# Six PSUM banks: three tiles of two banks each, or two-bank tiles in attention and one-bank tiles after it

## The chip, the cores and the metric

The kernel runs on one core of a Trainium2 chip. The metric is the device time of one execution in microseconds (us), the median of several executions. The engines are TensorE (PE, the matrix products; its weight loads are listed apart as PEld), VectorE (DVE), ScalarE (ACT), GpSimd (POOL) and SyncE (SP, which here issues DMAs).

## The reference

Attention feeds one mixture-of-experts-like layer, and that feeds a second one. All data are float32.

```python
def _attn_ref(q, k, v):                      # 2 x 12 heads x 448 x 64
    scores = scale * np.matmul(q, k.transpose(0, 1, 3, 2))
    scores = np.where(mask, -1000000000.0, scores)          # causal
    scores = scores - np.max(scores, axis=-1, keepdims=True)
    attn = np.exp(scores)
    attn = attn / (np.sum(attn, axis=-1, keepdims=True) + 1e-09)
    return np.matmul(attn, v)

def _moe_ref(x, w_in, w_out):                # 896 x 768, 768 x 2048, 2048 x 768
    r = np.maximum(x @ w_in, 0.0)
    return (r * r) @ w_out

def _moe2_ref(x, w1, w2, w3, w_out):         # 768 x 768 each
    h = np.maximum(np.maximum(x @ w1, x @ w2), x @ w3)
    return h @ w_out

x = attn_out.transpose(0, 2, 1, 3).reshape(896, 768)
return _moe2_ref(_moe_ref(x, ...), ...)
```

## The kernel before

**Stages.** The attention works on 12 pairs of heads. The two layers follow as four stages of block products: x by `w_in` (blocks f0 to f7, the "first stage" here), the squares by the first `w_out` (blocks o0 to o7, class `Second`, the second stage), that by w1, w2 and w3 with the maximum taken (blocks h0 to h8, the third stage), and the last `w_out`, whose products are partly in the order and partly in fixed code behind it (lines 1118 to 1179). Stages overlap: the first products of f0 and f1 stand between the last heads.

**Products.** Each block of two by two sub-blocks is computed with seven products M1 to M7 of sums of operands instead of eight plain ones, and each operand is a high and a low part, so that every product is three passes (`PASSES`): high by high, high by low, low by high. M1 to M7 of one block are 9 matmuls each of 128x448 (3 passes, 3 steps of depth), written by `matmul_in_parts` (L581). Beside a product stand the steps that feed it: a quarter of a weight is read as it came or summed (T), its high part is made by a copy on ACT (H, L199) or POOL (H', L289), its low part by a subtraction on DVE (L, `dve_lo`, L202). These quarters sit in a ring of five buffers (`wq`). Raw weights are cast (C on ACT, C' on POOL) and joined (J, DVE), and J sets the next load going. The steps that empty a bank are V: ACT copies (`keep`, L613, and L618, which goes from one bank into another), ACT relu and square (L640), or sums on DVE (`dve`, L212).

**PSUM.** The memory that PE writes has eight banks here. Six are held as three tiles of two banks each: pp0 (banks 0 and 1), pp2 (2 and 3), pp4 (4 and 5); banks 6 and 7 are tiles of their own, ps6 and ps7. In attention a pair holds the scores of one query block for both heads, or the transposed probabilities, which ACT or DVE copies out in one instruction over both banks (`place`, L499); the last pair of heads uses pp2 and pp4 alone for the latter. Afterwards the products use all eight banks singly, the six as halves of the pairs:

- the first stage gives each block three banks, b, c and d: even blocks 6, 1, 0 and odd ones 2, 4, 3; M5 and M3 go to c, M2 to d, the others to b;
- the second stage uses banks 5, 7, 6 (B) and 0, 1, 3 (C), the third 2, 5, 4 for even and 6, 7, 1 for odd blocks;
- the fixed code at the end uses 0, 3, 1 (`bb`), 7, 2, 5 (`cc`) and 4, 6 (`rest`).

**Order.** Nothing is scheduled by the compiler. `ORDER` is a string of 1776 step names, run one after the other (L1108); each engine gets its instructions in that order and runs them one after the other. Between instructions that use the same tile the layer below puts semaphore waits: a reader waits for the writer, and a writer waits for the readers before it. It does that by tile, so the halves of pp2 count as one thing in it. The names in the string: s scores, m mask and minimum (DVE, L450), e exponential (ACT, L458), a guard of the sum (DVE, a' on POOL, L465), r reciprocal, n norm (POOL, n' DVE, L473), g transposes (L484), h place, w product with V (L509), x and d operands of the first stage, then C, J, T, H, L, M and V as above, S, XH, XL and Y the second stage's operands and results, Z and W those of the last. A mark ' is the other engine for the same step; the number is the pair of heads, or the block.

Of the kernel before, what the change touches and what calls it, by code (L numbers as in the profile page):

```python
# [8 lines left out]
F32 = mybir.dt.float32  # L9
# [19 lines left out]
s2.0 m2.0 s0.0 m3.0 e2.0 e3.0 s4.0 m1.0 s6.0 m0.0 e1.0 m4.0 m5.0 a1'.0 r1.0 e4.0 e5.0 m6.0 s2.1  # L29
e0.0 n2.0 n3.0 s0.1 m2.1 m0.1 s6.1 m1.1 e6.0 m3.1 a2.0 g1.0 a0'.0 s4.1 m6.1 r0.0 n6.0 n4'.0 s6.2  # L30
g3.0 n5.0 m4.1 r2.0 e0.1 e1.1 h1.0 g0.0 e3.1 a2'.1 m5.1 e6.1 r2.1 e5.1 m6.2 n1.1 h3'.0 n1.0 n0.0
s4.2 m4.2 e4.1 h0.0 m5.2 a0'.1 r0.1 n0'.1 e6.2 n5.1 s6.3 g2.0 e2.1 e4.2 a1'.1 s0.2 h2'.0 s2.2 m0.2
s0.3 m1.2 e5.2 e0.2 n4.1 m2.2 g2.1 n6.1 m3.2 m1.3 a0'.2 m0.3 h2.1 w0.0 g0.1 e0.3 r1.1 n2'.1 r0.2
s4.3 h0'.1 n3.1 e1.3 s2.3 e3.2 m4.3 m5.3 g1.1 w1.0 e2.2 w2.0 w3.0 m3.3 m2.3 a1.2 n6.2 e1.2 h1.1
g3.1 g3.2 wload n4.2 e3.3 a2'.3 n5.2 r1.2 a2'.2 n2.2 e5.3 r2.2 g0.2 h3.1 e4.3 m6.3 n0.2 n3.2 s6.4
h3'.2 g1.2 s2.4 h0.2 h1.2 xh'.0 s0.4 xl.0 xf'.0 n1.2 e2.3 g2.2 r2.3 w0.1 a1'.3 m3.4 e6.3 e3.4 m2.4
m0.4 r1.3 e2.4 m6.4 h2.2 a0'.3 s4.4 m1.4 n2.3 e0.4 s2.5 n3.3 n0'.3 e6.4 g1.3 a1'.4 w1.1 n1.3 w2.1
w3.1 m4.4 r0.3 m2.5 e4.4 n4.3 n6.3 e1.4 m3.5 s6.5 n5'.3 a2'.4 m5.4 g2.3 h1'.3 g3.3 e5.4 h2.3 r1.4
r2.4 d3.1 h3.3 g0.3 s4.5 C'.i0 h0.3 a0'.4 n2.4 3h'.1 m6.5 n0.4 s0.5 w0.2 e6.5 w1.2 n1'.4 w2.2 r0.4
w3.2 m4.5 n6.4 m1.5 m5.5 e4.5 m0.5 e3.5 J.i0 n3.4 n4.4 n5.4 e1.5 xh'.2 e5.5 g1.4 e2.5 a1'.5 g2.4  # L40
h1'.4 s6.6 a0.5 xf.2 xl.2 h2.4 r1.5 r0.5 g3.4 3l.1 h3.4 g0.4 s2.6 n2.5 n3.5 h0.4 e0.5 a2'.5 s4.6
s0.6 m2.6 m3.6 m4.6 m0.6 g1.5 m5.6 r2.5 n5.5 n4.5 n1'.5 e3.6 w0.3 w1.3 w2.3 n6.5 m6.6 e2.6 w3.3
m1.6 d2.3 g3.5 h3'.5 d1.3 n0.5 h1.5 e4.6 g0.5 e1.6 C'.i2 e0.6 xh.3 a1'.6 a2'.6 1h'.3 h0.5 g2.5
s6.7 e6.6 s2.7 h2.5 s4.7 m6.7 xl.3 e5.6 s0.7 w0.4 m3.7 r1.6 w1.4 r2.6 w2.4 n3.6 n2'.6 m2.7 n1.6
e3.7 m4.7 m5.7 n0'.6 w3.4 s0.8 a0'.6 e6.7 g2.6 e2.7 m1.7 e5.7 a1'.7 m0.7 r0.6 g1.6 2h'.3 r1.7 e1.7
xh'.4 m1.8 m0.8 e0.7 h2.6 n5.6 d4.3 s6.8 s2.8 n4.6 s4.8 n6.6 h1.6 m2.8 e0.8 xf.4 m3.8 e4.7 g0.6
h0.6 xl.4 g3.6 w0.5 m5.8 a2'.7 a0'.7 n2.7 r0.7 e1.8 4h'.3 w1.5 e2.8 m4.8 w2.5 r2.7 w3.5 e3.8 h3.6
a2'.8 n4'.7 n5.7 1l.3 e5.8 s4.9 m6.8 d3.5 r2.8 J.i2 a1'.8 n3.7 g0.7 m5.9 r1.8 s6.9 n6.7 m4.9 e6.8
g3.7 n1.7 n0'.8 e4.8 3h'.5 n0.7 n2.8 h0.7 a0.8 r0.8 H'.f0M1 h3.7 w0.6 g2.7 n3'.8 g1.7 s2.9 e4.9
m6.9 n1.8 2l.3 n6.8 e5.9 n4.8 h2.7 h1.7 H'.f1M1 w1.6 w2.6 w3.6 m2.9 3l.5 m3.9 s0.9 g1.8 e6.9 s2.10  # L50
a0'.9 m1.9 xh.6 m0.9 xl.6 r0.9 m3.10 n5.8 h1.8 e1.9 e0.9 m2.10 n6'.9 H'.f1M2 s6.10 a2'.9 g3.8
C'.i1 s4.10 xf.6 h3.8 g2.8 g0.8 L.f1M1 e3.9 m6.10 w0.7 e3.10 e2.10 w1.7 r2.9 m5.10 n4.9 m4.10 w2.7
# [97 lines left out]
def tile_attention_moe_moe(  # L150
# [23 lines left out]
    nc = tc.nc  # L174
# [455 lines left out]
    class First(Sevens):  # L630
# [596 lines left out]
```

## Time and profile before

| | |
|---|---|
| median of 3 runs | 462.77 us (462.5 to 462.91) |
| profiled execution | 461.83 us, span of its profile 460.0 us |
| busy share of the span | PE 96%, DVE 85%, PEld 82%, ACT 63%, POOL 31% |
| mean granted clock of TensorE | 1.000 of full speed |
| DMA | 61.04 MB, mean 133 GB/s |

The span runs from the first instruction to the last; the time on record has 1.83 us more. Matmuls are pipelined and a row's duration includes some of the row before, so a busy PE is not a PE at its peak. An engine's busy share is a mean over stages with different limits; the windows below cut the span into stages.

### The profile page before, as it was taken

The page shows a single profiled execution, that of the slowest core. Times are in us where ns is not written, and L with a number is a line of the kernel's source. Part 1 is how long each engine was busy: PE and PEld are TensorE (multiplying, and loading weights), DVE is VectorE, ACT ScalarE, POOL GpSimd, SP SyncE. Part 2 cuts the span into 40 slices and gives each one's busy share as a digit, 9 for nine tenths or more (in the row PEclk, how much of TensorE's full clock was granted, in tenths as well). Part 3 has the DMA queues.
Part 4 walks back from the last instruction along what each step waited for, and adds up shares of the span by engine and source line. Part 5 has one row for each costly group of instructions (what it writes and reads, how often), then busy time and mean ns, then how long its engine had stood idle before and what let it go on. Part 6 is the DMA issues. An engine that isn't in the chain of part 4 may idle for free.

```text
span 460.0 us, 7587 instructions
## 1 busy us (share of the span) xinstructions
PE 441.3 (96%) x2585; PEld 378.0 (82%) x2585; DVE 392.1 (85%) x845; ACT 289.4 (63%) x652; POOL 143.2 (31%) x223
## 2 busy tenths in 40 slices
PE   8999999999899999999999999999999999899986
PEld 5555556888798998988999889888998999798986
DVE  6998998997777678989998999999898887779762
ACT  6998997756665798978756764763444443512541
POOL 4786998031012032234384113004221111100000
PEclk9999999999999999999999999999999999999999
DMA  7565553464764354896957552036273420000114
GB/s 222 175 192 166 177 185 93 146 198 137 207 176 118 122 152 129 223 212 178 186 87 146 196 200 76 27 111 205 70 216 126 139 68 2 0 1 0 51 37 154
DMA packets 42854, 61.04 MB, mean 133 GB/s; under 512 B 2112, under 2 KB 35008, under 8 KB 42816
## 3 DMA queue, kind: packets, MB, share of 16 engines
q1 hardware_dynamic: 39072, 55.61, 39.1%
q0 software_dynamic: 3456, 4.72, 6.5%
q8 instruction: 20, 0.33, 0.3%
q10 hardware_dynamic: 288, 0.23, 0.1%
q14 instruction: 18, 0.15, 0.1%
HBM read 53.08 MB, written 2.75 MB: 121 GB/s over the span
## 4 chain that ended last, share of the span: by engine, by line
PE 76%; ACT 9%; DVE 6%; POOL 4%; issue 2%; DMA 1%; ACTq 0%; POOLq 0%; SPq 0%; DVEq 0%
PE pp L581 43%; PE ps L581 21%; PE pp L1019 5%; ACT pr L458 4%; POOL pr L473 3%; PE ps L509 2%; PE pp L439 1%; DMA wr<-in_moe_w 1%; DVE wq L202 1%; ACT ph L499 1%; PE pp L484 1%; PE ps L1019 1%; DVE wd L273 1%; DVE z L212 1%; ACT up L263 1%
## 5 line engine op out<-in xcount | busy, mean ns | idle before, releaser
L581 PE MATMUL pp<-s,wq 128*128 128x448 f32 (+1 forms) x405 | 87.7, 364 | 5.4 <-ACT pp L618 2.9
L581 PEld LDWEIGHTS pp<-s,wq 128*128 128x128 f32 x405 | 74.0, 188 | 14.0 <-ACT pp L618 4.0
L581 PE MATMUL pp<-x,wq 128*128 128x448 f32 (+1 forms) x318 | 71.1, 365 | 1.2 <-DVE wq L202 1.1
L581 PE MATMUL pp<-a,wq 128*128 128x448 f32 x315 | 69.3, 368 | 1.8 <-ACT s L613 1.8
L289 POOL CAST wq<-wd 128x384 fp32r<-128x384 f32 x38 | 33.8, 890 | 107.1 <-PE ps L581 43.7
L581 PEld LDWEIGHTS pp<-x,wq 128*128 128x128 f32 x318 | 58.3, 188 | 8.6 <-DVE wq L202 2.9
L581 PEld LDWEIGHTS pp<-a,wq 128*128 128x128 f32 x315 | 58.7, 188 | 7.7 <-issue 1.5
L202 DVE TENSOR_TENSOR wq<-wd,wq 128x384 fp32r<-128x384 f32 x99 | 57.3, 591 | 7.6 <-ACT wq L199 5.3
L273 DVE SCALAR_TENSOR_TENSOR wd<-wr,up 128x768 int32<-128x768 int32 x56 | 55.0, 982 | 5.8 <-ACT up L263 4.2
L289 POOL CAST wq<-wt 128x384 fp32r<-128x384 f32 x29 | 17.0, 587 | 118.0 <-PE ps L581 46.8
L202 DVE TENSOR_TENSOR wq<-wt,wq 128x384 fp32r<-128x384 f32 x68 | 38.7, 581 | 11.5 <-POOL wq L289 7.2
L581 PE MATMUL ps<-s,wq 128*128 128x448 f32 (+1 forms) x224 | 48.3, 361 | 0.0
L458 ACT ACTIVATE pr<-pr,st 128x384 f32<-128x384 f32 (+3 forms) x84 | 43.8, 526 | 3.3 <-DVE st L450 3.3
L199 ACT CAST wq<-wd 128x384 fp32r<-128x384 f32 x61 | 31.0, 513 | 23.3 <-PE pp L581 14.6
L581 PE MATMUL ps<-x,wq 128*128 128x448 f32 (+1 forms) x200 | 44.4, 358 | 0.0
L581 PEld LDWEIGHTS ps<-s,wq 128*128 128x128 f32 x224 | 40.6, 188 | 4.0 <-DVE s L202 0.3
L473 POOL TENSOR_SCALAR pr<-pr,st 128x256 f32<-128x256 f32 (+3 forms) x68 | 41.4, 622 | 5.2 <-DVE st L469 4.0
L263 ACT CAST up<-wr 128x768 f16<-128x768 bf16 x27 | 29.2, 1083 | 21.5 <-DVE wd L273 7.6
L581 PEld LDWEIGHTS ps<-x,wq 128*128 128x128 f32 x200 | 36.4, 188 | 2.8
L581 PE MATMUL ps<-a,wq 128*128 128x448 f32 x144 | 32.2, 367 | 0.0
L450 DVE CUSTOM_DVE_ANT_0 pr<-pp,mask 128x384 f32<-128x384 f32 (+2 forms) x72 | 27.3, 416 | 4.9 <-PE pp L439 4.6
L199 ACT CAST wq<-wt 128x384 fp32r<-128x384 f32 x39 | 19.9, 513 | 17.0 <-PE pp L581 8.7
(166 smaller groups left out, 790.3 us busy)
## 6 DMA issues: line engine op xcount, KB each, us to landing
wr<-in_moe_w_out SPq DMA_DIRECT2D x22, 768.0 KB, 4.5
wr<-in_moe_w SPq DMA_DIRECT2D x18, 768.0 KB, 4.3
wr<-in_moe_w_in SPq DMA_DIRECT2D x16, 768.0 KB, 5.2
v<-in_v SPq DMA_DIRECT2D x12, 256.0 KB, 4.5
wd<-wd POOLq DMA_DIRECT2D x16, 192.0 KB, 5.1
q<-in_q SPq DMA_DIRECT2D x11, 256.0 KB, 2.9
out<-s SPq DMA_DIRECT2D x14, 192.0 KB, 1.9
k<-in_k SPq DMA_DIRECT2D x11, 224.0 KB, 3.8
```

The costliest lines, as they stand in the source:

```text
L199: nc.scalar.copy(hi, src)
L202: nc.vector.tensor_tensor(out=lo, in0=src, in1=hi.bitcast(F32), op=SUB)
L212: nc.vector.tensor_tensor(out=o, in0=a, in1=b, op=op)
L263: copy(self.up.bitcast(FH)[:, :, 1::2], self.top)
L273: nc.vector.scalar_tensor_tensor(out=self.t.bitcast(I32), in0=self.rest, scalar=13, in1=self.up.bitcast(I32), op0=ALU.logical_shift_right, ...
L289: copy(self.t[:, 0], self.src())
L450: nc.vector.tensor_tensor_reduce(out=self.pr[:, offs[u]:offs[u] + n], in0=self.sc[u][:, :n], in1=mask[:, mask.shape[1] - n:], scale=-SCALE ...
L458: nc.scalar.activation(sl, sl, ACTF.Exp, bias=self.st[:, 0, u:u + 1], scale=-1.0, accum_out=self.st[:, 1, u:u + 1],)
L473: engine.tensor_scalar(sl, sl, self.st[:, 2, u:u + 1], 1.0, op0=ALU.mult, op1=ALU.mult)
L509: nc.tensor.matmul(self.pv[r, kc * P:], self.n["v"][:, kc, r], self.ph[:, h, at], start=kc == 0, stop=kc == NK - 1,)
L581: nc.tensor.matmul(acc[:, c], w, x[:, c], skip_group_check=True, **flags)
L1019: nc.tensor.matmul(acc, a, b, start=start and i == 0 and e == 0, stop=i == KH - 1 and e == 2, skip_group_check=True,)
```

## The change

Pool code: the three pairs get pools of their own, opened so that they can be closed one by one. A new function `bank(n, w)` gives the tile of bank n. The first time that it is asked for a bank up to which the pairs still stand, it closes them in turn and opens a pool with two tiles of one bank each in the place of each, on the other side of the allocator and with waits by tile. So the first product in bank 0 or 1 closes pp0, and so on. The classes keep bank numbers and look the tile up when a step runs. `two_banks`, scores and probabilities are as before.

```diff
-    psp = ctx.enter_context(tc.tile_pool(name="psp", bufs=1, space=bass.MemoryType.PSUM))
-    pairs = [psp.tile([P, 2, 512], F32, name=f"pp{n}") for n in (0, 2, 4)]
-    ps = [t[:, i] for t in pairs for i in range(2)]
-    ps += [psp.tile([P, 512], F32, name=f"ps{n}") for n in (6, 7)]
+    def psum(name, stack=ctx, **kw):
+        return stack.enter_context(
+            tc.tile_pool(name=name, bufs=1, space=bass.MemoryType.PSUM, **kw)
+        )
+
+    psp = psum("psp")
+    ps = [None] * 6 + [psp.tile([P, 512], F32, name=f"ps{n}") for n in (6, 7)]
+    shared_by = [ExitStack() for _ in range(3)]
+    pairs = [
+        psum(f"pp{n}", shared_by[n]).tile([P, 2, 512], F32, name=f"pp{2 * n}") for n in (2, 1, 0)
+    ][::-1]
+
+    def bank(n, w=S):
+
+        while ps[n] is None:
+            i = ps.index(None)
+            shared_by[i // 2].close()
+            own = psum(f"psp{i}", side="right", reuse_waits="tile")
+            ps[i:i + 2] = [own.tile([P, 512], F32, name=f"ps{j}") for j in (i, i + 1)]
+        return ps[n][:, :w]
...
-            self.b, self.c, self.d, self.s = ps[b][:, :S], ps[c][:, :S], ps[d][:, :S], {}
+            self.banks, self.s = (b, c, d), {}
...
-            self.acc = {n: self.b for n in OPERANDS} | dict(M5=self.c, M3=self.c, M2=self.d)
+            self.acc = {n: "b" for n in OPERANDS} | dict(M5="c", M3="c", M2="d")
...
+        b, c, d = (property(lambda self, i=i: bank(self.banks[i])) for i in range(3))
...
-                        self.acc[n], self.q[n].t[:, ew, i], X[OPERANDS[n]][i][:, ex],
+                        getattr(self, self.acc[n]), self.q[n].t[:, ew, i], X[OPERANDS[n]][i][:, ex],
...
-            return (self.C if n in ("M2", "M5", "M3") else self.B)[m]
+            return bank((self.C if n in ("M2", "M5", "M3") else self.B)[m])
...
-    bb = [ps[n][:, :n2] for n in (0, 3, 1)]
-    cc = [ps[n][:, :n2] for n in (7, 2, 5)]
-    rest = [ps[n][:, :n2] for n in (4, 6)]
+    def bb(t):
+        return bank((0, 3, 1)[t], n2)
+
+    def cc(t):
+        return bank((7, 2, 5)[t], n2)
```

The `ORDER` string is new from its second step on. It has the same 1776 steps, but 144 names change engine: 80 weight casts go to POOL for 69 before (f blocks 26 for 27, o blocks 20 for 17, h blocks 34 for 25), 22 casts of raw weights for 19, and 26 guards for 30. The first line of it:

```diff
-s2.0 m2.0 s0.0 m3.0 e2.0 e3.0 s4.0 m1.0 s6.0 m0.0 e1.0 m4.0 m5.0 a1'.0 r1.0 e4.0 e5.0 m6.0 s2.1
+s2.0 m2.0 m3.0 s0.0 m1.0 e2.0 s4.0 m0.0 e3.0 e0.0 m4.0 s6.0 e1.0 a1'.0 s2.1 wload e4.0 s0.1 m5.0
```

What that does to the engines, at two places. First PE in the first stage, around product M2 of block f3, which goes to bank 3; the rows are output, operand, weight, shape and number of matmuls, each tile with a running number. Before, banks 2 and 3 are both pp2:

```order
L581 MATMUL pp2_69<-s2_1324,wq_1567 128x448 x3
L581 MATMUL ps6_71<-s2_747,wq_1552 128x448 x3
L581 MATMUL ps6_71<-s2_1078,wq_1552 128x448
L581 MATMUL ps6_71<-s2_1078,wq_1552 128x224 x2
L581 MATMUL ps6_71<-s2_1078,wq_1552 128x448
L581 MATMUL ps6_71<-s2_1324,wq_1552 128x448 x3
L581 MATMUL pp2_69<-a12_543,wq_1571 128x448 x3
L581 MATMUL pp2_69<-a12_933,wq_1571 128x448 x3
L581 MATMUL pp2_69<-a12_1285,wq_1571 128x448 x3
L581 MATMUL pp2_69<-s3_505,wq_1589 128x448 x3
```

The same place of the change, with the tiles of banks 0 to 5 as ps0 to ps5:

```order
L599 MATMUL ps2_1302<-s2_1348,wq_1576 128x448 x3
L599 MATMUL ps0_1209<-a12_593,wq_1590 128x448 x3
L599 MATMUL ps0_1209<-a12_936,wq_1590 128x448 x3
L599 MATMUL ps0_1209<-a12_1271,wq_1590 128x448 x3
L599 MATMUL ps4_1431<-s1_714,wq_1499 128x448 x3
L599 MATMUL ps4_1431<-s1_1313,wq_1499 128x448 x3
L599 MATMUL ps4_1431<-s1_1395,wq_1499 128x448 x3
L599 MATMUL ps3_1303<-a12_593,wq_1602 128x448 x3
L599 MATMUL ps3_1303<-a12_936,wq_1602 128x448 x3
L599 MATMUL ps3_1303<-a12_1271,wq_1602 128x448 x3
L599 MATMUL ps6_68<-s2_795,wq_1548 128x448 x3
```

The first line of each is the last of M6 into bank 2. Before, M6 of f2 stands between it and M2 into bank 3; now M2 of f2 (bank 0) and M5 of f3 (bank 4) do, and the tile that M2 of f3 writes is no longer the one that M6 wrote.

Second DVE near the end, around the last sum from the last product M3 of the third stage (block h8, bank 5); wol, wd and z2l are weights and operands of the last stage. Before:

```order
L212 TENSOR_TENSOR s_4306<-pp4_70,s_4306 128x448
L202 TENSOR_TENSOR wol5_4455<-wd_4331,woh5_4452 128x768
L212 TENSOR_TENSOR z5_4244<-z5_4244,s_4306 128x448
L202 TENSOR_TENSOR z2l4_4464<-z4_4205,z2h4_4460 128x896
L212 TENSOR_TENSOR wd_4331<-wd_4331,wd_3871 128x384
L212 TENSOR_TENSOR wd_4217<-wd_4217,wd_3731 128x384
L202 TENSOR_TENSOR z2l5_4470<-z5_4244,z2h5_4462 128x896
```

Of the change:

```order
L213 TENSOR_TENSOR s_4380<-ps5_1432,s_4380 128x448
L213 TENSOR_TENSOR z5_4244<-z5_4244,s_4258 128x448
L213 TENSOR_TENSOR z5_4244<-z5_4244,s_4426 128x448
L203 TENSOR_TENSOR z2l4_4489<-z4_4215,z2h4_4469 128x896
L213 TENSOR_TENSOR z5_4244<-z5_4244,s_4380 128x448
L203 TENSOR_TENSOR z2l5_4494<-z5_4244,z2h5_4492 128x896
L213 TENSOR_TENSOR z5_4244<-z5_4244,z2_3835 128x384
```

The low half of the weight (wol5, 128x768) and two sums of weights no longer stand between the sum and z2l5; two maxima into z5 have moved down in their place.

## Rows read from the trace of the kernel before

**Rows 1.** The page, busy us (share of the span) xinstructions of each engine
```profile
PE 441.3 (96%) x2585; PEld 378.0 (82%) x2585; DVE 392.1 (85%) x845; ACT 289.4 (63%) x652; POOL 143.2 (31%) x223
```

**Rows 2.** Busy time by stage: window, length, each engine, granted clock, DMA share, GB/s
```profile
core 0: us, PE busy (x) PEld busy (x) DVE busy (x) ACT busy (x) POOL busy (x), PEclk, DMA share, GB/s
0.00:76.00 76.00, 71.90 (x701) 43.44 (x702) 67.29 (x269) 67.35 (x213) 58.76 (x123) 1.00 0.59 183
76.00:160.00 84.00, 80.76 (x432) 70.26 (x431) 67.55 (x118) 53.57 (x103) 17.11 (x23) 1.00 0.51 151
160.00:200.00 40.00, 38.84 (x195) 35.21 (x194) 33.92 (x60) 36.12 (x78) 11.58 (x16) 1.00 0.63 170
200.00:240.00 40.00, 39.99 (x199) 36.50 (x200) 39.05 (x73) 28.10 (x59) 21.85 (x21) 1.00 0.76 160
...
280.00:320.00 40.00, 39.35 (x195) 35.18 (x194) 39.16 (x72) 22.32 (x43) 4.69 (x7) 1.00 0.28 88
```

**Rows 3.** Chain of waits from 0 to 86 us by line; PE's timeline there
```profile
by line: ACT pr L458 19.6%; POOL pr L473 15.6%; PE ps L509 11.3%; PE pp L439 6.7%; PE pp L581 6.2%; ACT ph L499 6.0%; PE pp L484 5.8%; issue 5.7%; DVE pr L450 3.2%; PE ps L1090 2.9%; POOL st L465 2.6%; PE ps L439 2.2%; POOL wq L289 1.7%; DV
...
82.91 1.95 PE L509 MATMUL ps<-ph,v 128*64 128x448 f32 x16
```

**Rows 4.** The chain's longest clean stretch (start, us); costliest group (busy, mean ns)
```profile
332.09 5.47 PE pp L581 x27
...
L581 PE MATMUL pp<-x,wq 128*128 128x448 f32 (+1 forms) x318 | 71.1, 365 | 1.2 <-DVE wq L202 1.1
```

**Rows 5.** PE's timeline: start, us, first matmul after a wait, [idle, releaser]
```profile
110.42 3.57 PE L581 MATMUL pp<-s,wq 128*128 128x448 f32 x17 [0.78 <-DVE wq L202]
...
117.03 2.08 PE L581 MATMUL pp<-a,wq 128*128 128x448 f32 x9 [1.20 <-ACT s L613]
...
119.75 0.47 PE L581 MATMUL pp<-s,wq 128*128 128x448 f32 x1 [0.63 <-ACT g L640]
...
144.72 1.49 PE L581 MATMUL pp<-a,wq 128*128 128x448 f32 x6 [0.62 <-ACT s L613]
...
180.89 2.30 PE L581 MATMUL pp<-s,wq 128*128 128x448 f32 x10 [1.07 <-ACT g L640]
...
317.12 1.09 PE L581 MATMUL pp<-s,wq 128*128 128x448 f32 x4 [0.60 <-ACT pp L618]
...
349.11 1.08 PE L581 MATMUL pp<-s,wq 128*128 128x448 f32 x4 [0.61 <-ACT pp L618]
...
395.23 2.12 PE L581 MATMUL pp<-s,wq 128*128 128x448 f32 x9 [1.70 <-ACT pp L618]
...
419.73 0.44 PE L1123 MATMUL pp<-woh,zr 128*128 128x384 f32 x1 [0.99 <-DVE s L212]
...
446.76 0.62 PE L1019 MATMUL pp<-piece,z2h 128*128 128x384 f32 x2 [1.38 <-ACT s L1046]
```

**Rows 6.** DVE's and ACT's timeline beside four of these waits
```profile
109.28 0.62 DVE L212 TENSOR_TENSOR g<-pp,s 128x448 f32<-128x448 f32 x1 [1.69 <-PE pp L581]
...
116.33 0.55 ACT L613 COPY s<-pp 128x448 f32<-128x448 f32 x1
...
392.83 0.61 DVE L212 TENSOR_TENSOR z<-pp,s 128x448 f32<-128x448 f32 x1
...
394.64 0.54 ACT L618 COPY pp<-pp 128x448 f32<-128x448 f32 x1
...
445.46 1.24 ACT L1046 COPY s<-pp 128x384 f32<-128x384 f32 x3 [4.11 <-PE pp L1019]
```

**Rows 7.** L202 by group (busy, mean ns); L465, duration ns min/median/max, first, last start
```profile
L202 DVE TENSOR_TENSOR wq<-wt,wq 128x384 fp32r<-128x384 f32 x68 | 38.7, 581 | 11.5 <-POOL wq L289 7.2 <-ACT wq L199 4.3
...
L465 POOL TENSOR_SCALAR st<-st x30: 218/228/576, 6.7 to 74.0; 128x2 f32<-128x2 f32 x20, 128x3 f32<-128x3 f32 x10
L465 DVE TENSOR_SCALAR st<-st x6: 154/164/478, 9.1 to 74.9; 128x2 f32<-128x2 f32 x4, 128x3 f32<-128x3 f32 x2
```

**Rows 8.** POOL's weight casts (ns min/median/max); DVE's waits for them: us, times, longest
```profile
L289 POOL CAST wq<-wd x38: 501/610/4467, 55.0 to 406.1; 128x384 fp32r<-128x384 f32 x38
...
DVE wq L202 <- POOL wq L289: 9.8, 13, 1.5
```

More of the change, by code (lines that the diff above doesn't have):

```diff
@@ L716, in tile_attention_moe_moe @@
     class Second:
[L721 to L722 removed]
+        B = 5, 7, 6
+        C = 0, 1, 3
         HALF = KH * P
@@ L1045, in keep @@
         o[n, t] = s_tile(n2)
-        nc.scalar.copy(o[n, t], bb[t])
+        nc.scalar.copy(o[n, t], bb(t))
     def store(rw, cs, t):
@@ L1055, in corner @@
     def corner(t):
-        product(bb[t], tiles(z1, 0, t), whole(0, left))
+        product(bb(t), tiles(z1, 0, t), whole(0, left))
     for t in range(TH):
@@ L1121, in tile_attention_moe_moe @@
         for e, (ex, ew) in enumerate(((0, 0), (0, 1), (1, 0))):
-            for acc, cs in zip(rest, (left, right)):
+            for acc, cs in zip((bank(4, n2), bank(6, n2)), (left, right)):
                 nc.tensor.matmul(
@@ L1132, in tile_attention_moe_moe @@
     for t in range(TH):
-        product(cc[t], lower(t), whole(KH, left))
+        product(cc(t), lower(t), whole(KH, left))
     for f in (KH + 1, KH + 2):
         s_1(f)
-    for t, cs in zip(rest, (left, right)):
+    for t, cs in zip((bank(4, n2), bank(6, n2)), (left, right)):
         r = s_tile(n2)
@@ L1145, in tile_attention_moe_moe @@
     for t in range(TH):
-        product(bb[t], halves("s2", t), pieces("t2"), False)
+        product(bb(t), halves("s2", t), pieces("t2"), False)
     for t in range(TH):
-        finish("s1", t, cc[t], t, left)
+        finish("s1", t, cc(t), t, left)
     for t in range(TH):
@@ L1151, in tile_attention_moe_moe @@
     for t in range(TH):
-        product(cc[t], halves("s1", t), pieces("t1"))
+        product(cc(t), halves("s1", t), pieces("t1"))
     s_half("s3", KH - 1)
@@ L1157, in tile_attention_moe_moe @@
     for t in range(TH):
-        product(bb[t], halves("s3", t), pieces("t3"), False)
+        product(bb(t), halves("s3", t), pieces("t3"), False)
     for i in range(KH):
@@ L1176, in tile_attention_moe_moe @@
     for t in range(TH):
-        product(cc[t], halves("s4", t), whole(KH, right), False)
+        product(cc(t), halves("s4", t), whole(KH, right), False)
     for t in range(TH):
-        finish("s2", t, cc[t], t, right)
+        finish("s2", t, cc(t), t, right)
 _INS = [
```

255 lines of the change are left out of this document (127 added, 128 removed).

## The prediction

> **What bounds the kernel now.** I read the page's busy shares first, then the busy time by stage, then every wait of PE in the timeline, then what ACT and DVE were doing beside each of those waits. PE is listed busy for 96% of the span and no other engine above 85% [rows 1]. By stage the picture splits. In the attention, whose last product ends at 84.86 us [rows 3] and which I take up to 76 us, before the first long blocks of the next stage, no engine is full: DVE, ACT and PE all show 67 to 72 us [rows 2], and the chain of waits there runs mostly through ACT's exponentials (L458) and POOL's normalisations (L473) [rows 3]. From 76 us on the kernel is one queue of products on PE. A clean stretch of 27 of them takes 5.47 us [rows 4], 203 ns from start to start, although each is listed at some 365 ns because the rows overlap [rows 4]. So a wait of PE costs its listed idle time plus about 0.16 us (365 less 203 ns), since the next product would have started before the last one's row ends.
>
> The timeline has ten waits of PE after 100 us that are over half a microsecond and involve the paired tiles [rows 5]. I looked at each for the banks. At 117.03 us the product M2 of block f3 starts: it writes bank 3, and it waited 1.20 us for an ACT copy (L613) that began at 116.33 and reads bank 2 [rows 5, 6]. Banks 2 and 3 are the two halves of tile pp2; nothing else joins the two instructions. At 395.23 us M3 of h6 goes into bank 5 and waits 1.70 us for ACT's copy L618 at 394.64, which goes from bank 2 into bank 4; what M3 truly needs, DVE's read of bank 5, had started at 392.83 and took 0.61 us, so it was over when PE fell idle [rows 5, 6]. At 446.76 us a product into bank 0 waits for the three ACT copies that start at 445.46, which themselves sat idle 4.11 us until PE had finished writing bank 1, the other half of pp0, though the first of them reads bank 0 [rows 6]. At 110.42 us the wait is second-hand: DVE stood 1.69 us before it read bank 1 at 109.28, held by a product into bank 0, and the weight that PE needed was queued behind it on DVE [rows 6, 5]. The waits at 119.75, 144.72, 180.89, 317.12, 349.11 and 419.73 us follow the same pattern (bank 2 against 3, 3 against 2, 1 against 0, 5 against 4, bank 2 held by a copy that itself waited on bank 5, bank 4 against 5).
>
> **The change part by part.** *The split tiles.* With one tile a bank these ten waits lose their cause. Their price, idle time plus 0.16 us each [rows 5]: in the first product stage 0.78 + 1.20 + 0.63 + 0.62 + 1.07 = 4.30, plus 5 x 0.16, is 5.1 us; in the third stage 0.60 + 0.61 + 1.70 = 2.91, plus 0.48, is 3.4 us; at the end 0.99 + 1.38 = 2.37, plus 0.32, is 2.7 us. Together 11.2 us, all on the engine that sets the end. What is late next, where these go, is a true reader of the same bank or a weight. In both orders at least one whole block of nine products (1.83 us at 203 ns) stands on PE between the product that fills a bank and the next product that goes over what ACT or DVE reads there, and the read takes about 0.6 us [rows 6]; so I expect no new wait of that kind, provided that the reader isn't stuck in its own queue.
>
> *The giving back.* The first product on banks 0, 2 and 4 waits until the last transposes in those pairs are copied out. That is needed before too, since both go through the same memory. It costs nothing if PE has other work there, and the order puts transposes or scores of the last pair between. Queued behind such a wait are the remaining P·V products on PE, and for them the last head's output. No row shows this wait in its new form; between a gain of nothing and a loss of one place copy by ACT, about 0.6 us, I take zero.
>
> *The new order, attention.* Counted in the two orders ahead of the last product of probabilities and V, DVE has 20 instructions of L202 and 15 of L212 where it had 18 and 14, and 10 guards where it had 6: 3 x 0.58 + 4 x 0.16 = 2.4 us more on DVE, and four guards, 0.9 us, less on POOL [rows 7]. DVE idles 8.7 us of these 76 [rows 2] and is hardly on the chain [rows 3], while POOL is; so I bound the attention's end between 0.9 us sooner and 2.4 us later, and take no change. PE has 24 products done by then instead of 27: 3 x 0.203 = 0.6 us later for what follows, which I count as a loss.
>
> *The new order, products.* The number of products is the same. Eleven more weight casts go to POOL (80 for 69), nine of them in the third stage; three more of the casts of raw weights too. POOL has room (it is idle most of the time after 160 us), and ACT gets freer. DVE's load is the same but for guards and copies that change places.
>
> *The second stage.* It gets its start 5.1 us sooner. From 200 to 240 us DVE is busy 39.05 of 40 us and from 280 to 320 us 39.16 [rows 2]; DVE cannot go faster there, so some of the time may be lost again as waits for DVE's low halves (L202). The loss lies between 0 and 5.1 us. From 160 to 200 us DVE has 6 us left over and from 76 to 160 us 16.4 [rows 2], enough to have the same work done 5 us sooner, so I take a value near zero, 1.2 us.
>
> *The end.* The code after the order string is the same. DVE's row after the last M3 is shorter by a 128x768 low half, so z2l of f5 should be there when PE asks for it; I take the 2.7 us whole.
>
> Sum: 11.2 - 0.6 - 1.2 = 9.4 us. The profiled execution took 461.83 us with a span of 460.0, so 1.83 us lie around it; its span would become 450.6 and its time 452.4. The median of the runs shown, 462.77, is 0.94 above the profiled one, and **462.77 - 9.4 = 453.4 us** is the forecast.
>
> **The rivals.** *DVE takes the first stage's gain back.* If DVE is what truly paces 160 to 320 us, all of the 5.1 us come back as waits for L202: 11.2 - 5.1 - 0.6 = 5.5 us gained, 457.3 us. For it speak 39.05 and 39.16 of 40 [rows 2]; against it that PE lost nothing to speak of between 200 and 240 us (39.99 of 40), so DVE kept up with a PE that never stopped. The Trainium skill, page "Perfetto Trace Analysis", section "Identifying the Most-Contended Engine", calls the engine of highest occupancy the bottleneck and judges TensorE by its weight loads rather than its matmuls. By that rule DVE with 85% against 82% of weight loads would be the engine to relieve [rows 1], and the time would be this rival's; the rows of the waits in the first stage, where PE stood for ACT and not for DVE's work, speak for PE there.
>
> *More comes back than the waits.* If nothing is lost in the second stage and the attention ends 0.9 us sooner, 11.2 - 0.6 + 0.9 = 11.5 us are gained and the time is 451.3; the low end of the range leaves 2.5 us more for an order that also shortens what is left of PE's waits. Against it: the rest of PE's waits are short, and an order that was rewritten whole makes some of its own.
>
> *POOL's casts hold up PE, and the kernel gets slower.* A cast on POOL takes 0.61 us in the middle and 4.47 us at the longest [rows 8], and DVE already waits 9.8 us for them in 13 places. With 11 more such casts, each that runs long costs 4.47 - 0.61 = 3.86 us where the product behind it has no other weight ready. Three on the path take 11.6 us and more than use up the 9.4; from there the kernel is slower, and four give 453.4 + 15.4 = 468.8 us. Against it: nine of the eleven are in the third stage, where DVE has more room, and the ring of five quarters lets a cast start some blocks ahead. The Trainium skill, page "SBUF — State Buffer", section "Who interferes with whom", says that a VectorE instruction with two SBUF inputs contends with a GpSimd instruction that reads SBUF. All the casts read SBUF and most of DVE's work has two inputs, which agrees with the spread from 0.50 to 4.47 us in the row, though the row doesn't show whose fault the long one is.
>
> *The change doesn't do what it says.* If the waits go by the memory of the old pair for longer than the handover, all ten stay and only the 0.6 us is seen: 463.4 us. The new tiles have names of their own in the order, which speaks against it.
>
> **How the numbers follow.** Forecast 0.60 (451.3 to 455.9), DVE takes it back 0.19 (455.9 to 459.5), more comes back 0.12 (448 to 451.3), nothing changes 0.03, slower 0.06. The range from 448.8 to 458.4 holds the first whole, most of the second and third, about 0.82; it takes in the bounds of the attention and of the second stage. Faster by over 0.2% (0.9 us, about what a measurement of this kernel can tell from no change): 0.60 + 0.19 + 0.12 = 0.91; within it 0.03; slower 0.06.
>
> **What would show it.** In the profile of the changed kernel PE's waits for ACT's L613, L618, L640 and L1046 copies and for DVE's sums (all under their new line numbers) should be nearly gone after 100 us, and the waits of ACT before its last copies (4.11 us) should split up. The last product of the attention should still end near 85 us [rows 3]. The second stage shows the first rival if PE's waits for DVE's low halves grow between 160 and 320 us; POOL's casts show the slower one if their longest come often and DVE's waits for them go well over 9.8 us. The forecast is wrong if the ten waits are still there, if the attention's end moves by more than 3 us, or if new waits of half a microsecond stand before products whose bank nobody else holds.

## The result, and the profile after

The changed kernel takes **446.69 us** (445.46 to 447.17, four runs) against 462.84 us (462.50 to 463.36) beside it: ratio 0.9646, interval 0.9625 to 0.9667. Beside the last kernels of the study it took 445.58 us against 462.69, ratio 0.964 (0.962 to 0.966). The direction was forecast; the gain, 16.2 us, is well over the 9.4 forecast, and the time lies 2.1 us under the range's low end of 448.8. One execution of e6, the profiled one, ran at a granted clock of 0.755 and took 530.79 us; it is left out below, and e6 has no row in the table.

The page of the kernel after, busy time of each engine, answers to [rows 1]; the profiled execution took 446.76 us with a span of 445.0:

```profile
PE 436.3 (98%) x2585; PEld 379.6 (85%) x2585; DVE 397.9 (89%) x848; ACT 286.1 (64%) x642; POOL 168.0 (38%) x230
```

PE does the same 2585 matmuls in a span that is 15.0 us shorter. The busy time by stage, in the columns of [rows 2]:

```profile
76.00:160.00 84.00, 83.48 (x439) 74.55 (x436) 72.34 (x122) 58.06 (x113) 18.45 (x25) 1.00 0.55 158
160.00:200.00 40.00, 40.00 (x201) 36.78 (x200) 37.56 (x68) 36.63 (x79) 17.09 (x16) 1.00 0.68 177
200.00:240.00 40.00, 39.16 (x196) 35.49 (x196) 39.05 (x69) 24.43 (x50) 19.66 (x22) 1.00 0.65 142
...
280.00:320.00 40.00, 40.00 (x202) 37.12 (x202) 38.77 (x70) 22.39 (x41) 19.07 (x11) 1.00 0.32 103
```

PE is nearly full from 76 us on but for 200 to 240 us, and DVE is busy 8.4 us longer before 200 us than it was (72.34 and 37.56 against 67.55 and 33.92). The chain of waits from 80 us on (start, us, what):

```profile
218.75 168.72 PE ps L599 x843
387.47 1.58 PE ps L1039 x9
389.05 5.53 PE ps L599 x28
```

From 218.75 us on the chain is PE's own queue, to the last sum, over 222.6 us. Before, it ran on PE alone for at most 42.6 us (349.11 to 391.70). The 27 products of [rows 4] are only one piece of such a stretch, and not the longest: the view starts a new piece where the tile's name changes, from pp to ps, and in the change all are ps. All of PE's waits with a releaser in the whole span (us in total, times, longest us):

```profile
PE pp L502 <- POOL pr L491: 1.9, 3, 0.9
PE ps L1113 <- DVE warm L1108: 1.2, 1, 1.2
PE ps L599 <- DVE wq L203: 0.8, 2, 0.4
PE pp L502 <- DVE st L468: 0.6, 1, 0.6
PE ps L599 <- ACT g L660: 0.3, 1, 0.3
```

Only the third and the last are in the block products. None of the ten of [rows 5] is left, nor any wait for ACT's copies; the last row is a product at 129.06 us that waits for ACT's relu, a true reader of its bank. ACT's wait of 4.11 us before its last copies [rows 6] is split up too: the three copies now start at 428.95, 430.46 and 432.02 us, behind 1.40, 1.04 and 1.08 us of idle time.

To count what PE loses I took the starts of its matmuls after the 24th block product, counting each of the nine matmuls of an M as one product (two halves of 224 columns are one): what a start is later than 0.203 us behind the one before it (0.175 for 384 columns, 0.110 for 224), where that is over 0.06 us. "24th" is when that product starts, and the next four columns are the loss by product number, up to 378 (three quarters of the first stage), to 1026 (about the end of the second), to 1575 (the last of the block products, with the gap behind it) and in the last stage's own code:

| kernel | median us | 24th at | to 378 | to 1026 | to 1575 | end | sum |
|---|---|---|---|---|---|---|---|
| before | 462.84 | 81.99 | 5.28 | 4.38 | 5.09 | 2.16 | 16.91 |
| after | 446.69 | 81.11 | 1.51 | 1.67 | 0.17 | 0 | 3.35 |
| after, second profile | 445.58 | 82.22 | 1.11 | 1.89 | 0 | 0 | 3.00 |
| e1 new tiles, old order | 449.24 | 81.89 | 1.05 | 3.86 | 0 | 0 | 4.91 |
| e2 old tiles, new order | 458.54 | 82.03 | 8.28 | 1.88 | 2.33 | 2.16 | 14.65 |
| e3 change, casts on old engines | 453.87 | 81.57 | 2.93 | 1.38 | 4.74 | 0 | 9.05 |
| e4 e1, attention in new sequence | 456.55 | 87.88 | 0.97 | 5.60 | 0 | 0 | 6.57 |
| e5 e1, banks 4 and 5 one tile | 455.15 | 81.92 | 0.85 | 4.62 | 5.10 | 0.52 | 11.09 |
| e7 change, 24 low halves twice | 460.40 | 80.87 | 1.05 | 16.41 | 0 | 0 | 17.46 |
| e8 change, three moves | 446.21 | 82.26 | 1.08 | 0.79 | 0 | 0 | 1.87 |
| e8, second profile | 447.43 | 82.11 | 0.97 | 3.55 | 0 | 0 | 4.52 |
| e9 e1, casts on new engines | 455.93 | 81.99 | 1.11 | 7.88 | 2.63 | 0 | 11.62 |

### The profile page after: what moved, and what is told of

It is laid out like the page before. It is cut to its first block, busy times and chain, and to the rows that moved or that the text cites. A ratio compares the mean times of both kernels' runs of the same rounds, so it can differ in the third digit from the quotient of the medians.

```text
span 445.0 us, 7593 instructions
## 1 busy us (share of the span) xinstructions
PE 436.3 (98%) x2585; PEld 379.6 (85%) x2585; DVE 397.9 (89%) x848; ACT 286.1 (64%) x642; POOL 168.0 (38%) x230
## 4 chain that ended last, share of the span: by engine, by line
PE 50%; DVE 1%; issue 0%
PE ps L599 41%; PE ps L1039 7%; PE ps L1146 1%; DVE wq L203 0%; DVE y L213 0%; DVE wd L274 0%; DVE g L213 0%; DVE s L213 0%
## 5 line engine op out<-in xcount | busy, mean ns | idle before, releaser
L599 PE MATMUL ps<-s,wq 128*128 128x448 f32 (+1 forms) x629 | 130.5, 361 | 0.0
L599 PEld LDWEIGHTS ps<-s,wq 128*128 128x128 f32 x629 | 115.3, 188 | 9.9 <-DVE s L203 0.4
L599 PE MATMUL ps<-x,wq 128*128 128x448 f32 (+1 forms) x518 | 104.0, 361 | 0.8 <-DVE wq L203 0.8
L599 PEld LDWEIGHTS ps<-x,wq 128*128 128x128 f32 x518 | 94.6, 188 | 9.6 <-DVE wq L203 2.1
L599 PE MATMUL ps<-a,wq 128*128 128x448 f32 x459 | 100.0, 367 | 0.3 <-ACT g L660 0.3
L599 PEld LDWEIGHTS ps<-a,wq 128*128 128x128 f32 x459 | 85.7, 188 | 8.4 <-issue 0.9
L476 ACT ACTIVATE pr<-pr,st 128x256 f32<-128x256 f32 (+3 forms) x84 | 44.0, 532 | 3.6 <-DVE st L468 3.0
L491 POOL TENSOR_SCALAR pr<-pr,st 128x128 f32<-128x128 f32 (+3 forms) x68 | 40.7, 612 | 8.7 <-DVE st L487 4.7
L468 DVE CUSTOM_DVE_ANT_0 pr<-pp,mask 128x256 f32<-128x256 f32 (+2 forms) x72 | 27.4, 413 | 4.4 <-PE pp L457 3.4
L502 PEld LDWEIGHTS pp<-ident,pr 64*128 64x128 f32 x384 | 15.4, 138 | 13.9 <-POOL pr L491 6.5
L203 DVE TENSOR_TENSOR x<-g,x 128x448 fp32r<-128x448 f32 x40 | 25.6, 654 | 0.7 <-ACT x L200 0.7
```

Source lines behind the costliest of these rows:

```text
L203: nc.vector.tensor_tensor(out=lo, in0=src, in1=hi.bitcast(F32), op=SUB)
L468: nc.vector.tensor_tensor_reduce(out=self.pr[:, offs[u]:offs[u] + n], in0=self.sc[u][:, :n], in1=mask[:, mask.shape[1] - n:], scale=-SCALE ...
L476: nc.scalar.activation(sl, sl, ACTF.Exp, bias=self.st[:, 0, u:u + 1], scale=-1.0, accum_out=self.st[:, 1, u:u + 1],)
L491: engine.tensor_scalar(sl, sl, self.st[:, 2, u:u + 1], 1.0, op0=ALU.mult, op1=ALU.mult)
L599: nc.tensor.matmul(acc[:, c], w, x[:, c], skip_group_check=True, **flags)
```

## The experiments

**Which part does it: tiles or order?** e1 takes the new pools and `bank()` with the order of before; e2 takes the new order with the old tiles.

```diff
 # e1: the changed kernel
-ORDER = (the change's)
+ORDER = (that of before)
 # e2: the kernel before
-ORDER = (that of before)
+ORDER = (the change's)
```

> The change's tiles with the order string of before, word for word. Theory T (the waits by tile are the cause, the order only adds): the ten waits, measured from start to start of PE's products in the trace of before, cost 12.3 us; they go, the rest of PE's waits (4.7 us after 80 us) and the attention stay. 462.8 - 12.3 = 450.5 us, taken as 449.5 to 452. Rival O (the new order is the cause): 458 to 463 us, since all but the tiles is before's.

Measured: 449.24 us, ratio 0.9696 (0.9679 to 0.9713), just under the 449.5 expected. (Ratios are to the kernel before, run beside each kernel: 462.69 to 463.16 us.) The tiles alone give some 14 us, and PE's loss falls from 16.91 to 4.91 us. What is left stands in the second stage. PE's timeline of e1 there (start, us, what, [idle, releaser]):

```profile
211.52 37.23 PE L598 MATMUL ps<-x,wq 128*128 128x448 f32 x186 [0.82 <-DVE x L202]
249.13 11.48 PE L598 MATMUL ps<-x,wq 128*128 128x448 f32 x56 [0.38 <-DVE wq L202]
261.30 0.88 PE L598 MATMUL ps<-x,wq 128*128 128x448 f32 x3 [0.69 <-DVE wq L202]
```

and DVE's, ahead of the first two:

```profile
203.61 1.03 DVE L212 TENSOR_TENSOR s<-wd 128x384 f32<-128x384 f32 x2 [1.83 <-DMA wd<-wd]
...
247.65 0.96 DVE L273 SCALAR_TENSOR_TENSOR wd<-wr,up 128x768 int32<-128x768 int32 x1 [1.44 <-ACT up L263]
```

DVE is late there because it stood in its own queue for a DMA (1.83 us) and for ACT's cast of a raw weight (1.44 us), and the operand that PE wanted was behind. The third wait comes from POOL's casts (last section).

> The tiles of before (three pairs) with the order string of the change. Theory T: products into one bank again wait for readers of the other one, and the new order keeps no distance between them, so it is no faster than before, 460 us or more, with PE's waits for ACT's and DVE's reads of the neighbour bank back and longer than before's. Rival O: the order alone brings most of the gain, 447 to 453 us.

Measured: 458.54 us, ratio 0.9902 (0.9886 to 0.9918). It is 12 us slower than the change, so the false waits are back; but it is 4.6 us faster than the kernel before beside it, which theory T had not expected. The new order on pairs loses more in the first stage (8.28 for 5.28 us) and less behind it. PE's timeline of e2 in the first stage:

```profile
106.29 2.06 PE L582 MATMUL pp<-s,wq 128*128 128x448 f32 x9 [1.19 <-ACT pp L619]
118.73 2.09 PE L582 MATMUL pp<-a,wq 128*128 128x448 f32 x9 [1.23 <-ACT s L614]
130.55 2.09 PE L582 MATMUL ps<-a,wq 128*128 128x448 f32 x9 [0.61 <-ACT s L614]
135.56 2.05 PE L582 MATMUL ps<-a,wq 128*128 128x448 f32 x9 [1.09 <-ACT g L641]
```

The first two are products into a pair that wait for ACT's copies, as in [rows 5]; the change, in the same order, has neither. The last two go into ps, the banks that were tiles of their own before too: there ACT comes late to a bank that it truly reads, and the change has 0.26 us of that left at 129.06 us. So not all of the 8.28 us is the pairs' own doing. In the third stage the new order happens to keep products away from the other half's readers even with pairs: the three waits of before there (0.60, 0.61 and 1.70 us) are gone in e2, so part of their price is counted in both parts. Hence 14 and 4.6 make 16 and not over 18.

**One pair's price.** e5 is e1 with banks 4 and 5 kept as one tile.

```diff
             own = psum(f"psp{i}", side="right", reuse_waits="tile")
+            if i == 4:
+                both = own.tile([P, 2, 512], F32, name="ps45")
+                ps[4:6] = [both[:, j] for j in range(2)]
+                continue
```

> As e1 (order of before, new tiles), but banks 4 and 5 stay one tile after attention. Theory T: the four waits of before that involve this pair (at 317.12, 349.11, 395.23 and 419.73 us) come back and no others; by the start-to-start gaps of PE in before they cost 0.88 + 0.88 + 1.97 + 1.26 = 5.0 us, so 449.2 + 5.0 = 454.2, taken as 453 to 455.5 us. If the waits don't add up like that (one hides the other, or a wait was due to the pair only by the profile), 449 to 452 us.

Measured: 455.15 us, 5.9 over e1, ratio 0.984 (0.9819 to 0.986). PE's timeline of e5:

```profile
311.81 2.09 PE L602 MATMUL ps<-s,wq 128*128 128x448 f32 x9 [0.61 <-ACT ps L641]
...
343.86 2.10 PE L602 MATMUL ps<-s,wq 128*128 128x448 f32 x10 [0.61 <-ACT ps L641]
...
389.84 5.75 PE L602 MATMUL ps<-s,wq 128*128 128x448 f32 x28 [1.71 <-ACT ps L641]
...
414.30 0.62 PE L1149 MATMUL ps<-woh,zr 128*128 128x384 f32 x2 [0.99 <-DVE s L212]
```

The four waits of [rows 5] on this pair return with their lengths to within 0.01 us (0.60, 0.61, 1.70, 0.99). This is the plainest evidence for the mechanism: the waits belong to the tile, and their prices add. By the starts the four cost 5.0 us; of the rest of the 5.9, 0.8 is in the second stage (4.62 for 3.86) and not theirs.

**The engines of the casts.** e3 is the change with its weight casts (H and C) on the engines of before; e9 is e1 with them on the engines of the change.

```diff
 # e3, one of 96 names; e9 does the reverse in the old order
-H'.h0M1
+H.h0M1
```

> The change whole, but every weight cast (H and C) on the engine on which it was before; the sequence of the steps stays. If the casts that went to POOL carry some of the gain, because ACT gets free earlier, it is slower than the change by 1 to 4 us, with PE's waits for weights grown in the second and third stage. If the engines of the casts don't matter (ACT has room, 64% busy), it is within 0.7 us of the change's 446.7.

Measured: 453.87 us, ratio 0.9799 (0.9771 to 0.9827), 7.2 over the change and so more than the 1 to 4 expected; and PE's longest waits are not for weights but for ACT. ACT's timeline of e3 before two waits:

```profile
306.78 0.51 ACT L199 CAST wq<-wt 128x384 fp32r<-128x384 f32 x1 [2.53 <-PE ps L598]
307.20 0.53 ACT L703 COPY z<-ps 128x448 f32<-128x448 f32 x1
...
391.38 1.08 ACT L263 CAST up<-wr 128x768 f16<-128x768 bf16 x1 [2.76 <-DVE wd L273]
392.32 0.93 ACT L199 CAST z2h<-z 128x896 fp32r<-128x896 f32 x1
393.16 0.82 ACT L199 CAST woh<-wd 128x768 fp32r<-128x768 f32 x1
393.89 0.52 ACT L637 COPY ps<-ps 128x448 f32<-128x448 f32 x1
```

and PE's, which they hold:

```profile
307.78 1.50 PE L598 MATMUL ps<-a,wq 128*128 128x448 f32 x6 [1.03 <-ACT z L703]
...
394.55 1.65 PE L598 MATMUL ps<-a,wq 128*128 128x448 f32 x7 [1.24 <-ACT ps L637]
```

A cast on ACT waits 2.53 us for a free buffer of the ring, which PE must give back, and the copy that empties PE's next bank is queued behind it. At 393.89 us the copy stands behind three casts, 2.8 us of work. With one tile a bank the wait is true, and what sets it is the queue of ACT.

> As e1 (order of before, new tiles), with every weight cast (H and C) on the engine that it has in the change; the counterpart of e3. If the choice of engines carries the order's share of the gain by itself, it is 2 to 3 us faster than e1's 449.2, 446 to 447.5. If engines and sequence are fitted to each other, so that only both together bring it, it is slower than e1, 450 to 456 us.

Measured: 455.93 us, ratio 0.9856 (0.9834 to 0.9878), 6.7 over e1. So neither the marks nor the sequence bring the order's share alone; they fit each other. PE's and DVE's timelines of e9 show most of it as one wait, and POOL's what is behind it:

```profile
208.31 10.04 PE L598 MATMUL ps<-x,wq 128*128 128x448 f32 x41 [3.52 <-DVE wq L202]
```

```profile
206.76 1.03 DVE L212 TENSOR_TENSOR s<-wd 128x384 f32<-128x384 f32 x2 [3.95 <-DMA wd<-wd]
```

```profile
195.38 0.84 POOL L289 CAST wq<-wd 128x384 fp32r<-128x384 f32 x1
197.14 1.27 POOL L289 CAST wq<-wd 128x384 fp32r<-128x384 f32 x1 [0.92 <-PE ps L598]
198.37 1.74 POOL L209 DMA_DIRECT2D wd<-wd  x2
```

POOL also issues the DMAs that add one weight to another (L209). In e1 the fourth of those behind 190 us was issued at 195.82 us and landed at 203.59; in e9 it stands behind the casts that the marks put on POOL, was issued at 198.90 and landed at 206.74, and DVE resumed at 206.76.

**The attention's sequence alone.** e4 is e1 with the attention's 516 steps in the sequence of the change, put in the places that attention steps had before.

```diff
 # e4: the changed kernel, its attention steps in the slots of the old order
-s2.0 m2.0 s0.0 m3.0 e2.0 e3.0 ...
+s2.0 m2.0 m3.0 s0.0 m1.0 e2.0 ...
```

> As e1 (new tiles, order of before), but the attention's steps stand in the sequence of the change, in the places that attention steps had before; the block products and all that feeds them stand as before. The change starts its 54th product 0.9 us and its first one 1.4 us sooner than before. If that is the attention's own sequence, this runs 1 to 2 us faster than e1. If it comes from what stands between the attention steps, it is within 0.5 us of e1 or slower.

Measured: 456.55 us, ratio 0.986 (0.9845 to 0.9875): 7.3 slower than e1, with the 24th product at 87.88 us; the attention, by the starts used below, takes 81.4 us for e1's 74.9. The sequence doesn't stand alone: what lies between the steps belongs to it. On the attention's share in the change it says nothing; that is read from the starts below.

**Has DVE room in the second stage?** e7 and e6 repeat a low half on DVE.

```diff
             dve_lo(self.t[:, 1], self.src(), self.t[:, 0])
+            if self.name[0] == "o" and self.name[2:] in TWICE:   # e7: M2, M6, M7; e6: M6
+                dve_lo(self.t[:, 1], self.src(), self.t[:, 0])
```

> The change, with the low halves of M2, M6 and M7 of all eight blocks of the second stage subtracted twice on DVE (the same result written again): 24 x 0.58 = 13.9 us more on DVE between about 190 and 290 us, each delaying its own product's weight by 0.58 us too. If DVE sets the pace of that stage in the change, as the rival in the prediction had it, nearly all is seen: 12 to 14 us slower, 459 to 461 us. If DVE has slack only in the trace's idle time from 160 to 320 us (6.2 us in the change), 13.9 - 6.2 = 7.7 us slower, 454.4. If work ahead of time hides most, under 4 us slower, below 450.7.

Measured: 460.40 us, ratio 0.9951 (0.9932 to 0.9969): 13.7 us more for 13.9 us of work. The windows of e7:

```profile
200.00:240.00 40.00, 35.35 (x164) 30.44 (x162) 37.02 (x68) 21.42 (x45) 16.89 (x18) 0.96 0.62 136
240.00:280.00 40.00, 36.04 (x174) 31.23 (x175) 39.26 (x67) 21.47 (x41) 15.50 (x17) 1.00 0.52 133
```

PE falls to 35 and 36 us of 40 there. About 1.4 us of the 13.7 is a fall of PE's clock (last section), so 12.3 are DVE's. In the changed kernel DVE has hardly any room in that stage, though PE shows none either.

> The change with only the low halves of M6 of the second stage's eight blocks subtracted twice: 8 x 0.58 = 4.6 us more on DVE, all between about 205 and 235 us. With 24 of them 13.7 us were paid for 13.9 us of work. If DVE sets the pace there outright, 4 to 5 us slower than the change, 450.5 to 452. If the stage has a few us of slack and the 24 paid extra because PE's clock fell in the long waits, 0 to 2 us slower, below 449.

Measured: 449.05, 449.40 and 452.41 us, ratio 0.9735 (0.9702 to 0.9769), so 448.9 to 452.0. The middle one is 3.8 us over the change measured beside it (445.58). Under 2 us, below 449, is all but ruled out; 4 to 5 fits, and the interval is too wide to say how much of the 4.6 us is hidden.

**Three moves for a better version.**

```diff
-XH.o1M1 C.i15 M4.f2 V1.f2M7 V0.f2M4 T2.f4
+XH.o1M1 M4.f2 V1.f2M7 V0.f2M4 C.i15 T2.f4
...
-S1.o5 J.o6r L.o2M6 V1.oM2 S1.o4 T3.o4 H.o3M5 XH.o1M5 M6.o0 V2.oM2 M6.o1 H.o3M6 L.o1M5 L.o3M6 XH.o4M6
+S1.o5 L.o2M6 H.o3M6 V1.oM2 S1.o4 T3.o4 L.o3M6 XH.o1M5 M6.o0 V2.oM2 M6.o1 H.o3M5 J.o6r L.o1M5 XH.o4M6
```

> The change with a few steps moved, for its three longest waits of PE after 100 us (0.42, 0.56 and 0.61 us from start to start, with 0.1 each behind them): the cast of raw weight i15 on ACT goes behind the relu of M2 or M4 of f2 that PE waits for, the high half of the weight of M6 of o3 goes ahead of that of M5, its low half ahead of DVE's sum before it, and the join of o6r behind both. If the waits are due to this order alone, 446.7 - 1.8 = 444.9 us, taken as 444.5 to 445.7. If DVE is late there anyway and only passes the wait on, 446.2 to 447.2 us.

Measured: 446.21 us (445.90 to 447.70). The three waits are gone in its profile (1.87 us lost for 3.35), but the time can't be told from the change's.

> The changed kernel as it is, beside the next one on the same chip: 445.5 to 447.2 us as in its first runs; its 24th product in the trace anywhere from 80.9 to 82.3 us, since five kernels with its attention showed that spread.

> The three moves once more. In the first profile PE's gaps after the attention fell from 3.35 to 1.40 us, but the 24th product started 1.15 us later than in the change's profile, and the medians differed by 0.5 us only. If the late attention was chance, the moves give 1 to 2 us against the change measured beside it. If the moves themselves make the attention later, within 0.5 us.

Measured side by side: the change 445.58 us (445.33 to 447.18), the three moves 447.43 (446.08 to 448.24). So they are no gain. In the second profile of the same program other waits stand in the second stage, PE's first and DVE's after it:

```profile
205.78 14.95 PE L599 MATMUL ps<-x,wq 128*128 128x448 f32 x73 [0.56 <-DVE x L203]
221.56 0.68 PE L599 MATMUL ps<-x,wq 128*128 128x448 f32 x2 [0.83 <-ACT wq L200]
```

```profile
204.63 0.56 DVE L203 TENSOR_TENSOR wq<-wd,wq 128x384 fp32r<-128x384 f32 x1 [2.60 <-POOL wq L290]
```

The loss up to product 1026 was 0.79 us in one execution and 3.55 in the other. Which wait one sees in that stage is partly chance, and a single profile is no ground for moves worth half a microsecond each. The 24th product came at 82.26 and 82.11 us, so the late start of the first profile is in both; the change's own two profiles have 81.11 and 82.22.

## Why the prediction was too small

**The mechanism was right.** The ten waits are gone with the tiles (e1), four of them come back with one pair (e5), and nothing took their place: PE has no wait for a bank in the third stage and behind it, and one of 0.26 us, for a true reader, ahead of it. At the end it was the tiles that did it and not DVE's shorter row: e1, with DVE's old row, loses nothing there, and e2, with the new one on pairs, still waits 0.78 us for DVE before the last stage. The point that a whole block of nine products stands between true users of a bank held. The giving back cost nothing that shows: no product of the change waits for a place copy.

**The price of the ten waits was a little low.** I took 11.2 us as idle time plus 0.16 us each. By the starts of the matmuls they cost 12.3: the product behind the first one after a wait is late too, by about 0.1 us, ten times.

**The step that failed is the price of the new order: a loss of 1.2 us in the second stage, where there was a gain.** I counted how many instructions each engine has in the two orders and found near nothing, then booked losses of 0.6 us (attention) and 1.2 (second stage). Yet the change is 2.6 to 3.7 us faster than e1 (446.69 and 445.58 against 449.24). Of the two losses, the 1.2 us was about right for the tiles alone: e1 loses 3.86 us in the second stage, before 4.38 with 1.34 in it for the wait at 180.89 us, so 0.8 came back. The new order then took about 2 us out of that stage (1.67 and 1.89 left), which my sum had no term for. Other profiles side with it, 1.88 and 1.38 with the new sequence (e2, e3) and 4.62 with the old (e5); but one program gave 0.79 and 3.55 there (e8), so the size is uncertain. e3 and e9 show where such time lies: in what is queued ahead of a copy on ACT, of a low half on DVE or of a DMA's issue on POOL, not in the engines' totals. I named that ACT "gets freer" with more casts on POOL, and priced it at zero; taking the casts back cost 7.2 us. But giving them to POOL in the old order cost 6.7, so what has a price is how casts and sequence fit, and not their number. Which moves of the new order bring the 2 us, no run shows.

**The attention.** I bounded it between 0.9 us sooner and 2.4 later and took no change, less 0.6 for three products that move behind it. From the 28th score matmul to the last product with V it takes 74.0 us in both profiles of the change and 74.9 in before and e1: the 0.9 us end of my bound. What in the order does that stays open, since e4 couldn't tell. With the three products behind it, 0.3 us of that stays. Ahead of that score, the same program starts 9.1 to 10.2 us into the span from run to run (before 9.7), so about 0.6 us of the difference between the two profiles is chance. The last product with V ends at 83.35 and 84.47 us in the two profiles, for 84.86 before. The change's row that answers to the last of [rows 3]:

```profile
81.40 1.95 PE L527 MATMUL ps<-ph,v 128*64 128x448 f32 x16
```

**The two accounts differ.** The profiled executions are 461.83 and 446.76 us, 15.1 apart; the medians are 16.2 apart. The profiled execution of before was 1.0 us under its median, and I subtracted a gain read from it from the median. For this pair of profiles the sum then goes: forecast 9.4, plus 1.1 (ten waits), plus about 2.5 (second stage, 1.2 booked as a loss and 1.3 gained), plus 0.9 (attention), plus 0.6 (chance of the start), plus 1.1 (profile against median) is 15.6 of 16.2; the rest is in gaps under 0.06 us, which the table leaves out (0.6 us by the same starts).

**The rivals.** *DVE takes the gain back*: no. In e1, with DVE's work in its old order, 0.8 of the 5.1 us came back, and DVE was busy 7.0 us longer ahead of 200 us (70.31 us from 76 to 160 and 38.20 from 160 to 200). But e7 shows that it is close: in the change the second stage has DVE and PE full together. The Trainium skill's rule (page "Perfetto Trace Analysis", section "Identifying the Most-Contended Engine") names DVE as the engine to relieve, before as after (85% against 82% of weight loads, now 89% against 85%). From before to e1 14 us came from tiles with DVE's 845 instructions unchanged, against the rule; in the second stage of the change e7 agrees with it. *More comes back than the waits*: this is what happened, and it got 0.12 and a floor of 448. *POOL's casts make it slower*: no, although they did get longer. In the change (duration ns min/median/max), answering to [rows 8]:

```profile
L290 POOL CAST wq<-wd x43: 500/747/12085, 47.4 to 391.0; 128x384 fp32r<-128x384 f32 x43
```

and DVE's wait for them:

```profile
DVE wq L203 <- POOL wq L290: 10.8, 17, 1.8
```

The longest took 12.1 us where it was 4.5, and DVE waits 10.8 us for 9.8. I had priced a long cast at its length; what it costs is the last section's subject.

## What to carry to other kernels

When the profile blames an engine for a wait, compare the banks or bytes that the two instructions touch with the tile that tracks them: ten waits here were between halves of a tile that shared nothing, and their prices added up nearly as read. Count a wait from start to start on the waiting engine, and read the gain against the same execution that the waits were read from. A new order of work can't be priced by counting instructions per engine; look at what stands in the queue ahead of each instruction that frees a buffer, and leave room in the range for a gain as well as for a loss.

## What the runs showed of the hardware

**A long cast on POOL waits for DVE; DVE pays some 0.3 us at its end.** POOL's and DVE's timelines of the kernel after, around the longest cast:

```profile
279.19 12.09 POOL L290 CAST wq<-wd 128x384 fp32r<-128x384 f32 x1 [6.88 <-PE ps L599]
291.22 0.50 POOL L290 CAST wq<-wt 128x384 fp32r<-128x384 f32 x1
```

```profile
290.27 0.63 DVE L203 TENSOR_TENSOR s<-y,s 128x448 fp32r<-128x448 f32 x1
290.81 0.63 DVE L213 TENSOR_TENSOR y<-y,ps 128x448 f32<-128x448 f32 x1
291.34 1.20 DVE L274 SCALAR_TENSOR_TENSOR wd<-wr,up 128x768 int32<-128x768 int32 x1
```

From 279 to 291 us DVE never paused, and all its instructions had two inputs in SBUF; the cast ended 0.5 us after the first one that reads PSUM instead (290.81). Up to there DVE's rows keep their length (0.6 us, 0.95 for 128x768); the next one, beside POOL's next cast, takes 1.20 for 0.95. Another cast, and the low half that needs it:

```profile
189.72 3.25 POOL L290 CAST wq<-wd 128x384 fp32r<-128x384 f32 x1 [3.06 <-PE ps L599]
```

```profile
191.98 0.63 DVE L203 TENSOR_TENSOR x<-g,x 128x448 fp32r<-128x448 f32 x1
193.00 0.56 DVE L203 TENSOR_TENSOR wq<-wd,wq 128x384 fp32r<-128x384 f32 x1 [0.40 <-POOL wq L290]
```

The cast of 3.25 us ends 0.4 us after DVE comes to a stop for it: DVE pays 0.40 us, and not the 3.25. In e1 both together make PE's wait of 0.69 us before 261.30 us (POOL's rows, then DVE's):

```profile
258.22 1.67 POOL L289 CAST wq<-wd 128x384 fp32r<-128x384 f32 x1 [4.96 <-DVE x L202]
259.84 1.06 POOL L263 CAST up<-wr 128x768 f16<-128x768 bf16 x1
```

```profile
259.92 1.32 DVE L202 TENSOR_TENSOR wq<-wd,wq 128x384 fp32r<-128x384 f32 x1 [0.40 <-POOL wq L289]
```

DVE waits 0.40 us for the first cast, and its low half then takes 1.32 us for 0.55, beside a cast of a raw weight. This is no exception. In the change 46 of DVE's 562 rows behind 84 us are over 0.12 us longer than the median of their kind (operation, shape and output), by 0.31 us in the middle and 15.5 us together, and a cast runs on POOL beside each of them; before, it is 30 rows and 10.6 us, again with a cast beside each. So most of the 5.8 us that DVE is busier in the change is this, and 2.4 us of it lie between 200 and 320 us (6.1 for 3.7), where e7 finds hardly any room on DVE. The Trainium skill, page "SBUF — State Buffer", section "Who interferes with whom", says that such DVE instructions contend with GpSimd's reads, which agrees; the rows add that POOL was held while DVE went on, and DVE for some 0.3 us a time. It was read from rows, not tried by itself.

**The clock fell after a wait of PE.** The windows of e7 around one of its longest waits (1.99 us of listed idle time before 223.11 us):

```profile
220.00:224.00 4.00, 2.01 (x9) 1.37 (x8) 3.96 (x8) 2.51 (x5) 1.71 (x2) 1.00 0.19 42
224.00:228.00 4.00, 3.85 (x12) 2.96 (x12) 3.96 (x9) 0.98 (x2) 0.03 (x1) 0.57 1.01 246
```

The granted clock, 1.00 before, has a mean of 0.57 in the four microseconds behind it, between the two levels of 2.4 and 1.2 GHz (1.00 and 0.50), and products start 0.373 us apart for 0.203. In e9 the same followed its wait of 3.52 us, with a mean of 0.71 from 208 to 212 us and 0.87 in the next four, and in e4 a wait of 1.95 us before 69.00, with 0.71 from 68 to 72. In before and after, whose longest listed waits are 1.70 and 1.17 us, it is 1.00 throughout. About 1.4 us of e7's 13.7 is this, an estimate: eight products, each 0.17 us late.
